# A strided load of 127 rows becomes one of 128 rows, and one row is replaced behind the flip

## The chip, the cores and the metric

The kernel runs on one core of a Trainium2 chip. The metric is the device time of one execution in microseconds (us), and lower is better. The program has five engines that run their own instruction streams: TensorE (PE in the profile, with PEld for its weight loads), VectorE (DVE), ScalarE (ACT), GpSimd (POOL) and SyncE (SP), which here only issues transfers.

## The reference

The reference takes `x` of shape (8, 3008, 256) and two weight matrices. It computes the real part of a two-dimensional discrete Fourier transform over the sequence (3008) and the channels (256) of each of the 8 batches, and puts the 24064 resulting rows through a two-layer network with an ELU between:

```python
X = np.fft.fft(np.fft.fft(x, axis=1), axis=2).real
h = X.reshape(24064, 256) @ w_in            # 256 x 2048
g = np.where(h > 0, h, np.exp(np.minimum(h, 0)) - 1)
out = g @ w_out                             # 2048 x 256
```

`x` is float32. The weights come as float64, and the kernel converts them itself, chunk by chunk, with integer and float operations on VectorE, ScalarE and GpSimd.

## The kernel before

The transform over the sequence is done as matrix products with cosine and sine tables (tiles `MC`). Since cosine is even and sine is odd, rows s and 3008 - s, and rows counted from the middle, 1504, are first added or subtracted ("folded"), so that about a quarter of the rows is left to multiply. The results go to the rings `Rr`, `Ir` and `Rb`, and the network reads its columns from there: matrix products into the PSUM tiles `H`, an ELU on DVE, ACT and POOL into `G`, and the second product into the four accumulators `pA` to `pD`. After the first batch this is one long stream of matrix products. The next batch's rows are loaded and folded underneath it.

The change lies in the load of batch 0, before that stream can begin. Four tiles `xl0` to `xl3` of 128 partitions hold six rows of 256 channels in each partition:

- `xl0` and `xl3` are read ascending from row 0 and from row 1504. Their first four rows per partition are called `x0a` and `x3a`, their last two `x0b` and `x3b`.
- `xl1` and `xl2` are read from the second half and from the first half of the sequence, and are to be used in descending order. Two of their six rows per partition, `x1b` and `x2b`, are gathered in descending order by GpSimd. Their four-row parts `x1a` and `x2a` are read in ascending order, and TensorE then turns the partitions round by a product with a flipped identity matrix (`flip`), function `turn`: the result is a PSUM tile `H`.

`first_folds` names the steps. `t3a`, `t3b`, `t0a` and `t0b` are the four turns: `t3*` turns parts of `xl2`, which belong to `xl3`, and `t0*` turns parts of `xl1`, which belong to `xl0`. `a` stands for rows 1 and 3 of a partition, `b` for rows 0 and 2. The mirrors `y3a`, `y3b`, `y0a`, `y0b` on DVE add the turned rows to `xl3` and `xl0` (channels reversed), and `y3c` and `y0c` do the same with the gathered rows. `Za`, `Zb` and `Zc` add `xl0` and `xl3`, `Zd` and `Ze` (GpSimd) subtract them, `ea` to `ec` fold the channels, and `x-odd1`, `R-odd1` and so on are the first products with the tables. `w0a` to `w0M` convert the first chunk of weights.

Why `x1a` has 127 rows: partition 127 of `xl1` would begin at row 3005 of batch 0 and hold rows 3005, 3006, 3007 and 3008. Row 3008 is row 0 of the next batch, where the fold wants row 0 of this batch. So `load_first` (line 696) loads 127 partitions on SP, and ScalarE's queue issues two small transfers for partition 127: three rows (3 KB) and row 0 (1 KB).

The order is written out by hand: the string `FRONT` lists the steps, and the events are sorted and emitted in that order. Each engine executes its own part of it in order. For SP the list gives

`x2a x3a fl x1a x0a x3b x0b m0c m0a m0b m0d w0g cc m1 pk w1g m2 w2g w5g u0g ...`

where `fl` is the flip matrix, `m*` are tables, `w*g` and `u*g` chunks of weights and `cc` and `pk` small tables. TensorE begins with 13 keep-warm products on zeros, then `t3b t3a t0a t0b`, then 11 more keep-warm products (`d3 d8`), then `x-odd1`. DVE's order is `y3b y3a y0a y3c y0c Za y0b ea`. The PSUM tag `H` has three buffers.

The framework gives the transfers of SP and ScalarE eight semaphores in turn. An issue therefore waits for the landing of the eighth such transfer before it. In the kernel before, `w0g` uses the semaphore of `x1a` and `cc` that of `x0a`.

Of the kernel before, what the change touches and what calls it, by code (L numbers as in the profile page):

```python
# [17 lines left out]
SEQ = 3008  # L18
ND = 256
# [162 lines left out]
def kernel(  # L182
# [7 lines left out]
    nc = tc.nc  # L190
# [26 lines left out]
    def xrows(b, row, step, n, rows=6):  # L217

        return bass.AP(
            tensor=xt,  # L220
            offset=x.offset + (b * SEQ + row) * ND,
            ap=[[step * ND, n], [1, rows * ND]],
        )
# [373 lines left out]
    def bank(tag):  # L597
        bufs = 3 if tag == "H" else 1
        return ppool.tile([128, 512], FP, tag=tag, bufs=bufs, name=tag)

    def mm(out_, lhsT, rhs, start, stop=True):
        pin(
            nc.tensor.matmul(  # L603
                out_, lhsT=lhsT, rhs=rhs, start=start, stop=stop, skip_group_check=True
            )
        )

    def vtt(o, a, b, op):
        pin(nc.vector.tensor_tensor(out=o, in0=a, in1=b, op=op))  # L609

    def gtt(o, a, b, op):
        pin(nc.gpsimd.tensor_tensor(out=o, in0=a, in1=b, op=op))  # L612

    def act(o, i, func=AF.Copy, **kw):
        pin(nc.scalar.activation(out=o, in_=i, func=func, **kw))  # L615
# [78 lines left out]
    def load_first(L, j, few):  # L694

        if few or j in (0, 3):
            L_loads[j, few]()
            return
        n = 128 if j == 2 else 127
        row = (HALF if j == 2 else SEQ) - 511  # L700
        nc.sync.dma_start(out=L[j][0:n, 2 * ND :], in_=xrows(0, row, 4, n, 4))
        if j == 1:
            for c, r, m in ((2, SEQ - 3, 3), (5, 0, 1)):
                nc.scalar.dma_start(
                    out=L[j][127:128, c * ND : (c + m) * ND],
                    in_=xrows(0, r, 4, 1, m),
                )

    def first_folds(L):

        flip = spool.tile([128, 384], FP, tag="side", bufs=2, name="flip")[:, 0:128]
        rows = [t.rearrange("p (m d) -> p m d", d=ND) for t in L]
        plus, minus = rows[1][:, ::-1], rows[2]
        eo = [
            [
                spool.tile(
                    [128, 768], FP, tag=f"{k}{1 + 2 * kodd}", bufs=1, name=k
                )
                for k in "eo"
            ]  # L720
            for kodd in range(2)
        ]
        ops = {}

        turned = {}

        def turn(j, m):
            ps = turned[j, m.start] = bank("H").rearrange("p (m d) -> p m d", d=ND)
            mm(ps, flip, rows[(1, 2)[j == 3]][:, ::-1][:, m], True)

        def mirror(j, m):
            own = rows[j]
            if m is rest:
                other = rows[(1, 2)[j == 3]][:, ::-1][:, m]
            else:
                other = turned[j, m.start]
            vtt(own[:, m, 1:], own[:, m, 1:], other[:, :, :0:-1], ALU.add)
            vtt(own[:, m, 0:1], own[:, m, 0:1], other[:, :, 0:1], ALU.add)

        def fold(kodd, ri, m, tt):  # L740
            src = minus if kodd else plus
            lo, hi = (
                t.rearrange("p m (d o) -> p m o d", o=2)
                for t in (src[:, m, 1:129], src[:, m, 255:127:-1])
            )
            o = eo[kodd][ri].rearrange("p (m o d) -> p m o d", o=2, d=64)[:, m]
            if ri:
                tt(o, lo, hi, ALU.subtract)
            else:
                tt(o, lo[:, :, ::-1], hi[:, :, ::-1], ALU.add)  # L750

        def edge(kodd, m, copy):
            src = minus if kodd else plus
            o = eo[kodd][0].rearrange("p (m o d) -> p m o d", o=2, d=64)[:, m]
            copy(o[:, :, 0, 63:64], src[:, m, 0:1])

        def vcopy(o, i):
            pin(nc.vector.tensor_copy(out=o, in_=i))

        def add(m):  # L760
            vtt(plus[:, m], rows[0][:, m], rows[3][:, m], ALU.add)

        def even(m):
            fold(0, 0, m, vtt)
            edge(0, m, vcopy)

        near, odd, even_, rest = slice(0, 4), slice(1, 4, 2), slice(0, 3, 2), slice(4, 6)
        every = slice(0, 6)
        for key, m in (("a", odd), ("b", even_), ("c", rest)):
            for j in (0, 3):  # L770
                if m is not rest:
                    ops[f"t{j}{key}"] = lambda j=j, m=m: turn(j, m)
                ops[f"y{j}{key}"] = lambda j=j, m=m: mirror(j, m)
            ops["Z" + key] = lambda m=m: add(m)
            ops["e" + key] = lambda m=m: even(m)
        ops["oab"] = lambda: fold(0, 1, near, vtt)
        ops["oc"] = lambda: fold(0, 1, rest, vtt)
        for key, c in (("Zd", slice(0, 3 * ND)), ("Ze", slice(3 * ND, 6 * ND))):
            ops[key] = lambda c=c: gtt(L[2][:, c], L[0][:, c], L[3][:, c], ALU.subtract)
        ops["em"] = lambda: fold(1, 0, every, vtt)  # L780
        ops["cm"] = lambda: edge(1, every, act)
        ops["om"] = lambda: fold(1, 1, every, gtt)
        ops["fl"] = lambda: nc.sync.dma_start(out=flip, in_=FL_dr.ap())

        def keep():
            d = state["x_odd"] = spool.tile([128, 6], FP, tag="xd", bufs=1, name="xd")
            act(d.unsqueeze(2), minus[:, :, 128:129])

        ops["xd"] = keep
        return eo, plus[:, :, 128], ops  # L790
# [209 lines left out]
    class Dft:  # L1000
# [16 lines left out]
        def copy(self):  # L1017

            M, h = self.M, (self.n + 1) // 2
            self.anti = spool.tile([128, NH], FP, tag="anti", bufs=2, name="anti")  # L1020
            act(self.anti[0:M, 0:h], self.even[0:M, h : 2 * h])
# [674 lines left out]
    exp_neg(warm)  # L1696
    L_first, L_loads = load_x(0)
    EO, x_first, ops = first_folds(L_first)

    R_even, I_even = (Dft(ri, 0, 0, EO[0][ri]) for ri in range(2))  # L1700
# [42 lines left out]
    for j in range(4):  # L1743
        for few in range(2):
            names[f"x{j}{'ab'[few]}"] = lambda j=j, few=few: load_first(L_first, j, few)
# [209 lines left out]
    for n in range(16):  # L1955
        j, k = divmod(n, 4)
# [65 lines left out]
    for b in range(2, NB):  # L2022
# [35 lines left out]
        for n in range(4):  # L2058
            ri, m = divmod(n, 2)
            rel(46 + n, 1.3, quarter_pairs, b, ri, 0, 1 + m)  # L2060
        for n, step in enumerate((43, 44, 45, 46, 51, 53)):
            ri, m = divmod(n, 3)
# [65 lines left out]
```

## Time and profile before

| what | value |
|---|---|
| median of 3 runs | 1931.41 us (1931.06 to 1931.83) |
| the profiled execution, its own time | 1932.27 us |
| span of its profile | 1930.5 us |
| TensorE, busy | 1902.0 us, 99% |
| VectorE, busy | 1465.3 us, 76% |
| GpSimd, busy | 1352.9 us, 70% |
| ScalarE, busy | 878.0 us, 45% |
| mean TensorE clock granted | 0.995 |

The profile is of one execution. Its times are counted from the start of the span; the execution's own time is 1.8 us longer than the span. "L603" is line 603 of the kernel, which for a product is the line of the helper `mm`; likewise all DVE additions carry L609 and all ACT operations L615, so steps are told apart by their tiles and shapes. "Idle before" is what the engine waited before an instruction, and the name behind the arrow is what ended the wait. "SPq" is SyncE's instruction stream, in which issues of transfers stand.

### The profile page before, as it was taken

Reading aid. Unit: us, or ns where it says so; the run is one execution under the profiler, and the core shown is the slowest. Engines: PE = TensorE matmul, PEld = TensorE weight load, DVE = VectorE, ACT = ScalarE, POOL = GpSimd, SP = SyncE. Lnnn points to the kernel's source line nnn. Section 1 sums busy time; section 2 is a strip of 40 time slices with the busy share of each in tenths; the row PEclk is TensorE's granted clock in tenths of the full one; section 3 lists DMA queues with packets and bytes.
Section 4 is the critical chain, followed back from the end, with each engine's and each line's share of the span. In section 5 each row is a group of like instructions: output and inputs, shape, how many; then the busy total and the mean of one; then the engine's idle time right before and its main releaser. Section 6 shows DMA issues by size and latency. Waiting matters only on the chain.

```text
span 1930.5 us, 27900 instructions
## 1 busy us (share of the span) xinstructions
PE 1902.0 (99%) x8966; PEld 1650.3 (85%) x8966; DVE 1465.3 (76%) x2789; ACT 878.0 (45%) x1710; POOL 1352.9 (70%) x1835
## 2 busy tenths in 40 slices
PE   5999999999999999999999999999999999999999
PEld 2788888888888888888888888888888888888887
DVE  3876667778787887878877887877877778767666
ACT  1774444444444444444444444444444444444443
POOL 1798767777677776877668786677766777556554
PEclk7999999999999999999999999999999999999999
DMA  5534421211011111110201111012110210100101
GB/s 193 188 20 29 43 47 36 57 36 32 16 33 43 32 40 20 35 44 20 44 15 46 38 25 39 12 42 49 30 27 12 56 20 17 17 12 12 22 10 25
DMA packets 278806, 73.87 MB, mean 38 GB/s; under 512 B 253891, under 2 KB 268998, under 8 KB 278660
## 3 DMA queue, kind: packets, MB, share of 16 engines
q1 hardware_dynamic: 270304, 62.69, 16.4%
q0 software_dynamic: 6176, 9.13, 1.5%
q8 instruction: 71, 1.16, 0.3%
q14 instruction: 75, 0.61, 0.1%
q10 hardware_dynamic: 2180, 0.27, 0.1%
HBM read 47.17 MB, written 24.80 MB: 37 GB/s over the span
## 4 chain that ended last, share of the span: by engine, by line
PE 96%; DVE 1%; DMA 1%; ACT 1%; SPq 1%; issue 0%; POOL 0%; ACTq 0%; DVEq 0%; POOLq 0%
PE H L603 37%; PE pB L603 17%; PE pC L603 17%; PE pD L603 17%; PE pA L603 9%; DMA xl<-in_x_dram 1%; SPq L276 1%; ACT G L615 0%; ACT Wsc L615 0%; DVE xl L609 0%; ACT pow L615 0%; POOL w L612 0%; DVE v L609 0%; PE M L603 0%; DVE pow L475 0%
## 5 line engine op out<-in xcount | busy, mean ns | idle before, releaser
L612 POOL TENSOR_TENSOR G<-G 128x256 f32<-128x256 f32 x1437 | 1046.0, 737 | 501.4 <-DVE G L1419 342.4
L615 ACT ACTIVATE G<-H 128x512 f32<-128x512 f32 x376 | 224.6, 597 | 917.8 <-DVE G L1403 917.8
L1389 DVE SCALAR_TENSOR_TENSOR E<-Rb,wex,H 128x256 f32<-128x256 f32 x752 | 327.9, 477 | 334.7 <-PE H L603 329.6
L603 PE MATMUL H<-Rr,Wsc 128*128 128x256 f32 x1504 | 387.3, 380 | 0.0
L603 PE MATMUL H<-Ir,Wsc 128*128 128x256 f32 x1504 | 386.6, 379 | 0.3 <-DVE E L1389 0.3
L603 PE MATMUL pC<-G,WT 128*128 128x256 f32 x1440 | 369.5, 379 | 0.0
L603 PEld LDWEIGHTS H<-Ir,Wsc 128*128 128x128 f32 x1504 | 278.4, 189 | 47.9 <-DVE E L1389 2.4
L603 PEld LDWEIGHTS H<-Rr,Wsc 128*128 128x128 f32 x1504 | 282.1, 190 | 40.7 <-issue 2.1
L603 PEld LDWEIGHTS pC<-G,WT 128*128 128x128 f32 x1440 | 273.6, 190 | 37.2
L1403 DVE SCALAR_TENSOR_TENSOR G<-E,H 128x512 f32<-128x512 f32 x376 | 257.2, 684 | 41.7 <-POOL G L612 11.5
L1419 DVE SCALAR_TENSOR_TENSOR G<-G,H 128x512 f32<-128x512 f32 x376 | 256.1, 681 | 39.5 <-ACT G L615 39.5
L1419 DVE SCALAR_TENSOR_TENSOR G<-M,G 128x512 f32<-128x512 f32 x376 | 257.2, 684 | 1.2 <-ACT M L615 1.2
L615 ACT ACTIVATE G<-G 128x512 f32<-128x512 f32 x376 | 233.5, 621 | 0.1
L603 PE MATMUL pD<-G,w 128*128 128x256 f32 x784 | 229.4, 379 | 0.0
L603 PE MATMUL pA<-G,w 128*128 128x256 f32 x784 | 229.4, 379 | 0.0
L603 PE MATMUL pB<-G,w 128*128 128x256 f32 x784 | 229.3, 379 | 0.0
L615 ACT ACTIVATE M<-G 128x512 f32<-128x512 f32 x376 | 223.9, 596 | 0.9 <-DVE G L1403 0.9
L615 ACT ACTIVATE M<-M 128x512 f32<-128x512 f32 x376 | 221.2, 588 | 0.1
L603 PE MATMUL pB<-G,WT 128*128 128x256 f32 x720 | 214.3, 379 | 0.0
L603 PE MATMUL pD<-G,WT 128*128 128x256 f32 x720 | 214.1, 379 | 0.0
L603 PEld LDWEIGHTS pA<-G,w 128*128 128x128 f32 x784 | 148.9, 190 | 20.6 <-DVE G L1419 0.3
L603 PEld LDWEIGHTS pB<-G,w 128*128 128x128 f32 x784 | 148.9, 190 | 20.4 <-PE H L603 0.2
(169 smaller groups left out, 1561.7 us busy)
## 6 DMA issues: line engine op xcount, KB each, us to landing
out_dram<-ot SPq DMA_DIRECT2D x496, 32.0 KB
xq<-in_x_dram SPq DMA_DIRECT2D x48, 94.0 KB
out_dram<-ot SPq DMA_DIRECT2D x256, 2.0 KB
Rb<-r SPq DMA_DIRECT2D x10, 376.0 KB
raw<-in_moe_w_in_dram SPq DMA_DIRECT2D x7, 512.0 KB
MC<-dft_mats SPq DMA_DIRECT2D x3, 943.5 KB
xl<-in_x_dram SPq DMA_DIRECT2D x5, 512.0 KB
xq<-in_x_dram SPq DMA_DIRECT2D x12, 192.0 KB
```

What stands on the lines that cost most here:

```text
L276: nc.sync.dma_start(out=L[j][:, 0 : 4 * ND], in_=xrows(b, row, 4, 128, 4))
L603: nc.tensor.matmul(out_, lhsT=lhsT, rhs=rhs, start=start, stop=stop, skip_group_check=True)
L612: pin(nc.gpsimd.tensor_tensor(out=o, in0=a, in1=b, op=op))
L615: pin(nc.scalar.activation(out=o, in_=i, func=func, **kw))
L1389: nc.vector.scalar_tensor_tensor(out=S.E[:, c], in0=Rb[:, cols(i)], scalar=wex[:, f : f + 1], in1=S.H[:, c], op0=ALU.mult, op1=ALU.add,)
L1403: nc.vector.scalar_tensor_tensor(out=two(S.G[:, 0:512])[:, :, ::-1], in0=two(S.E), scalar=2.0, in1=two(S.H), op0=ALU.mult, op1=ALU.subtract,)
L1419: nc.vector.scalar_tensor_tensor(out=o, in0=e, scalar=-1.0, in1=h, op0=ALU.add, op1=ALU.max)
```

## The change

`x1a` is loaded like `x2a`, with all 128 partitions by one transfer on SP. Partition 127's fourth row is then row 3008 of the batch sequence, which is row 0 of batch 1. The two small transfers on ScalarE's queue go away. After the flip that row lies in partition 0, first row group, of the PSUM tile that `t0b` writes. There ScalarE overwrites it with row 0 of batch 0 from `xl0`, before the mirror `y0b` reads the tile.

```diff
@@ load_first
-        n = 128 if j == 2 else 127
         row = (HALF if j == 2 else SEQ) - 511
-        nc.sync.dma_start(out=L[j][0:n, 2 * ND :], in_=xrows(0, row, 4, n, 4))
-        if j == 1:
-            for c, r, m in ((2, SEQ - 3, 3), (5, 0, 1)):
-                nc.scalar.dma_start(
-                    out=L[j][127:128, c * ND : (c + m) * ND],
-                    in_=xrows(0, r, 4, 1, m),
-                )
+        nc.sync.dma_start(out=L[j][:, 2 * ND :], in_=xrows(0, row, 4, 128, 4))
@@ first_folds, turn
             ps = turned[j, m.start] = bank("H").rearrange("p (m d) -> p m d", d=ND)
             mm(ps, flip, rows[(1, 2)[j == 3]][:, ::-1][:, m], True)
+            if j == 0 and m.start == 0:
+                act(ps[0:1, 0], rows[0][0:1, 0])
```

The rest of the program is the same, instruction by instruction on each engine. Since two transfers fewer take a semaphore, the turn of the eight moves by two: `m0a` now waits for `x2a`, `m0b` for `x3a`, `m0d` for `fl`, `w0g` for `x1a`, `cc` for `x0a`, `m1` for `x3b`, `w1g` for `m0c`, `m2` for `m0a` and `w2g` for `m0b`.

## The prediction

> **What bounds the kernel now.** I read the page first: the busy shares, the slices and the chain that ended last.
>
> ```profile
> PE 1902.0 (99%) x8966; PEld 1650.3 (85%) x8966; DVE 1465.3 (76%) x2789; ACT 878.0 (45%) x1710; POOL 1352.9 (70%) x1835
> PE   5999999999999999999999999999999999999999
> PEclk7999999999999999999999999999999999999999
> PE 96%; DVE 1%; DMA 1%; ACT 1%; SPq 1%; issue 0%; POOL 0%; ACTq 0%; DVEq 0%; POOLq 0%
> ```
>
> The whole is bound by TensorE, except in the first slice (48 us), which is half empty and where the granted clock is low. A microsecond saved before the stream of products starts shifts all of it, since the 96% of the chain behind it is products one after another. So I next asked for busy time in stretches of the beginning. The columns are stretch, length, busy time of PE, PEld, DVE, ACT and POOL, granted clock, DMA share and GB/s.
>
> ```profile
> 3.00:6.00 3.00, 3.00 (x9) 1.06 (x7) 0.00 (x0) 0.00 (x0) 0.96 (x1) 1.00 1.02 391
> 7.00:14.00 7.00, 1.45 (x4) 0.38 (x2) 1.42 (x4) 0.00 (x0) 0.00 (x0) 0.95 0.06 26
> 14.00:23.00 9.00, 0.00 (x0) 0.00 (x0) 0.00 (x0) 0.00 (x0) 0.00 (x0) 0.50 0.69 211
> 26.00:29.00 3.00, 0.00 (x0) 0.00 (x0) 0.00 (x0) 0.00 (x0) 0.00 (x0) 0.50 0.07 27
> 30.00:34.00 4.00, 4.00 (x7) 1.23 (x6) 2.43 (x7) 0.00 (x0) 0.19 (x1) 0.53 0.80 256
> 34.00:42.00 8.00, 7.27 (x31) 4.45 (x29) 7.86 (x15) 0.72 (x1) 3.88 (x2) 1.00 0.93 332
> 80.00:1930.00 1850.00, 1846.65 (x8758) 1613.25 (x8756) 1418.72 (x2690) 846.54 (x1651) 1322.88 (x1803) 1.00 0.17 31
> ```
>
> From 7 to 14 us and again from 26 to 29 us the transfers move 26 or 27 GB/s at a share of 0.06 or 0.07, which is one of 16 engines. All five compute engines stand still. The timelines of TensorE, SP and VectorE (start, length, instruction, idle before and what ended it) say who waits:
>
> ```profile
> 6.57 1.88 PE L603 MATMUL H<-xl,flip 128*128 128x512 f32 x4
> 29.49 3.75 PE L603 MATMUL H<-xl,flip 128*128 128x512 f32 x4 [21.04 <-DMA xl<-in_x_dram]
> 33.03 2.93 PE L603 MATMUL M<-zero 128*128 128x512 bf16 x11
> ...
> 2.22 0.33 SPq L701 DMA_DIRECT2D xl<-in_x_dram  x1
> 2.60 11.38 SPq L276 DMA_DIRECT2D xl<-in_x_dram  x1
> 29.37 0.39 SPq L403 DMA_DIRECT2D raw<-in_moe_w_in_dram  x1
> ...
> 8.49 1.42 DVE L609 TENSOR_TENSOR xl<-xl,H 128x510 f32<-128x510 f32 x4 [7.41 <-PE H L603]
> 31.57 0.76 DVE L609 TENSOR_TENSOR xl<-xl,H 128x510 f32<-128x510 f32 x2 [21.66 <-PE H L603]
> 32.24 2.02 DVE L609 TENSOR_TENSOR xl<-xl,xl 128x510 f32<-128x510 f32 x5
> 34.19 0.74 DVE L609 TENSOR_TENSOR xl<-xl,H 128x510 f32<-128x510 f32 x2
> ```
>
> t3b and t3a run at 6.57 us; t0a waits 21.04 us for a transfer of xl and starts at 29.49. That transfer is x1a, issued at 2.22: 508 KB, or 520 KB of a thousand bytes, at 27 GB/s are 19.3 us, which is the time from about 6.5 us, when the rest of what was issued has landed, to the DMA packets' last semaphore of this load at 28.95. The next issue on SP, x0a, takes 11.38 us, because part of it goes to the engine that is full. Even what lands elsewhere stays incomplete: of the later loads' packets the trace has 120 of 128 early and the last 8 only after 30 us. w0g is issued at 29.37, right after x1a landed, whose semaphore it uses. x2a, from the same line but with 128 rows, is in the tile before 6.57. The 22 us are thus x1a on one engine, and not a lack of bandwidth.
>
> **What the skill says.** "DMA: Bandwidth & Descriptors", section "Why a DMA increments its semaphore by 16 and not by 1", says that a transfer from SP is split over the largest k up to 16 that divides the slowest dimension of both sides, with 127 partitions giving 1 and 128 giving 16. The trace agrees: x1a moves at 27 GB/s, and 391 GB/s is moved with x2a and x3a in flight. The same page, "Queues, rings and completion order", says that on each DMA engine descriptors are consumed in ring order; the last 8 packets of each later load, after 30 us, agree. "TensorE: Matmul & The Clock Gate", part 1, says that the clock halves after about 3.4 us without work and needs as long of work to return; here it is 0.50 from 14 us on and 1.00 from 34. No price is taken from the skill.
>
> **The change part by part.**
>
> Removed: two issues on ScalarE's queue, 0.53 and 0.24 us at 0.75 and 1.38 us. ScalarE's next real work is at 40.13 us, so this is worth nothing; they land long before x1a.
>
> x1a on 16 engines: I add up what must move, at the 391 GB/s of 3 to 6 us. 1.41 MB had moved by 6.0 us (3 us at 80 GB/s, 3 at 391), so the line begins at 6.0 - 1.41/0.391 = 2.4 us. In MB of a thousand KB, with the gathers x1b and x2b beside the queue: x1a is complete at 2.16 MB, x0a at 2.69, x3b 2.95, x0b 3.21, m0a 3.79, m0d 4.18, w0g 4.70, m1 5.86, w1g 6.41, m2 7.37, w2g 7.90. (The trace of before moved 7.9 MB up to 44 us, where SP's next batch starts.) That gives landings at 7.9, 9.3, 9.9, 10.6, 12.1, 13.1, 14.4, 17.4, 18.8, 21.3 and 22.6 us. From landing to the product it took 0.54 us before (28.95 to 29.49). The turn of eight semaphores holds nothing up: each issue needs a landing several microseconds before the queue runs dry (m0a needs x2a, w0g needs x1a at 7.9, w2g needs m0b at about 12.6).
>
> TensorE: t0a can start at the end of t3a, 8.45 us, or at 7.9 + 0.5; it ends at 9.4, since at full clock four passes took 1.88 (before: 3.75 at half clock). t0b ends at 10.3. DVE's y0a needs x0a, 9.3 + 0.5 = 9.8 us, and starts there instead of at 31.57. y3c needs x3b at 10.4, y0c x0b at 11.1; with 0.7 us for each mirror they start at 10.5 and 11.2, so they wait for nothing. Za ends at 12.5 instead of 34.26. The shift is 21.8 us.
>
> Does what follows keep it? All of it between 32 and 78 us stands in the chain as DVE, PE, ACT and POOL, without a transfer. Each need, moved by 21.8, against its landing plus 0.5: m0a 35.80 to 14.0 against 12.6; w0g 39.68 to 17.9 against 14.9; m1 42.52 to 20.7 against 17.9; w1g 43.62 to 21.8 against 19.3; w2g 46.66 to 24.9 against 23.1. The slack is 1.4 to 3 us. Behind that, SP was held before by the conversion of the first chunk, to 43.2 us, so its later issues move with the compute; the queue drains at 22.6 where the moved schedule begins to fill it at 44.2 - 21.8 = 22.4: 0.2 us late.
>
> The added copy on ScalarE: the nearest row is the same operation between SBUF tiles,
>
> ```profile
> L615 ACT ACTIVATE xl<-xl 1x256 f32<-1x256 f32 x1 | 0.4, 399 | 0.0
> ```
>
> so 0.4 us, from 10.3 (t0b) to 10.8. Its reader y0b comes after Za at 12.5 in DVE's order, so y3c, y0c and Za hide it. Without that cover it would cost 0.4 plus a hand-over, 0.5 us. The copy adds a wait at the head of ScalarE's stream; queued behind it is the first conversion step, at 40.13 before and 18.3 moved. Writing to PSUM isn't shown here for this shape; I bound it by 0.2 and 0.6 us (a 128x6 copy took 0.215, a 128x512 one out of PSUM 0.597), both hidden. x0's reload for batch 1 now also waits for this copy, at about 51 us before, 30 moved: nothing.
>
> Sum: -21.8 + 0.2 = -21.6, at most -22.2 (y0a at 9.4, with x0a in time), on 1932.27, the profiled execution: 1910.7. That execution is 0.86 above the median, so the median becomes 1909.8; I say 1910.0.
>
> **The rivals.**
>
> Transfers become the bound. If the packets flow at 256 GB/s, as in the stretch 30 to 34, and not at 391, x0b is in at 2.4 + 3.21/0.256 + 0.5 = 15.4 (4.2 late) and w2g at 33.7 instead of 24.9, 8.8 late: the gain shrinks to 13 us, 1918.4. At 332 (34 to 42) it is 1.8 less: 1911.8. For it: the stretch 14 to 23 shows 211. Against: there one engine of 16 was out and SP itself stalled, and 44 to 62 us holds 383 with the same kinds of loads.
>
> The load doesn't spread, because something other than the count keeps it on one engine: 1931.4, no change. Against: x2a, same line, same strides.
>
> Slower: the dense stretch starts with a clock below 1.00, for instance because the long rest at half clock was what allowed it. 1% of clock on 1846.65 us of products is 18.5 us, so the gain is gone when the mean falls under 0.988; at 0.98 the time is 1931.4 - 21.4 + 37 = 1947. Against: 1.00 is granted over all of 80 to 1930 us.
>
> The copy is late after all (y0b waits): gain less 0.5 to 1, 1910.8.
>
> **How the numbers follow.** Full shift 0.75 (its own range 1908.5 to 1912.5), late copy 0.06, transfers as bound 0.14 (1912 to 1925, most of it below 1918), doesn't spread 0.03, slower 0.02. The forecast is 1910.0. The range 1908.0 to 1917.0 holds the first two and over half of the third; below lies the bound -22.2 with the runs' spread of 0.4. About 0.2% (3.9 us) is what a measurement of this kernel can tell from no change: faster 0.95, same 0.03, slower 0.02.
>
> **What would show it.** Right: SP's issues 2 to 8 within a few us without the 11 us one; DMA near 390 GB/s from 3 to 22 us with no stretch of 26; t0a directly behind t3a near 8.5 us at clock 1.00; y0a near 9.8; ScalarE's copy of 1x256 near 10.5 with y0b behind Za; x-odd1 near 14; the dense stretch 21 to 22 us earlier and the same length. Wrong: t0a again after 20 us (it doesn't spread); DVE or PE waiting on transfers of MC or raw between 10 and 25 us (bandwidth); a clock below 1.00 after 34 us.

## The result, and the profile after

The changed kernel takes 1913.61 us (median of 6 runs, 1911.99 to 1916.05), against 1931.39 us (1931.06 to 1931.83) for the kernel before. The ratio is 0.9908 with a 95% interval of 0.9896 to 0.9921: 0.9% faster. The profiled execution took 1911.99 us, its span is 1910.2 us; against the profiled execution before that is 20.3 us less.

The page of the changed kernel: the slices of TensorE and its clock, and the chain by engine.

```profile
PE   8999999999999999999999999999999999999999
PEclk9999999999999999999999999999999999999999
PE 97%; DVE 1%; ACT 1%; DMA 0%; issue 0%; POOL 0%; SPq 0%; ACTq 0%; DVEq 0%; POOLq 0%
```

The first slice went from 5 to 8 tenths, and the low clock in it is gone. The shares of DMA and of SP's queue in the chain have fallen from 1% each to below half a percent. One piece of DMA is left in the chain's first 110 us, the wait up to the landing of x0a (start, length):

```profile
2.62 8.42 DMA xl<-in_x_dram
```

Busy time by stretch (length, then PE, PEld, DVE, ACT and POOL, granted clock, DMA share, GB/s):

```profile
3.00:6.00 3.00, 3.00 (x9) 1.05 (x7) 0.00 (x0) 0.00 (x0) 0.96 (x1) 1.00 0.94 339
6.00:10.00 4.00, 3.23 (x9) 1.16 (x7) 1.30 (x4) 0.00 (x0) 0.00 (x0) 1.00 0.98 359
10.00:14.00 4.00, 3.66 (x15) 1.35 (x13) 2.99 (x10) 0.38 (x1) 0.64 (x1) 1.00 1.04 398
18.00:22.00 4.00, 4.00 (x18) 2.92 (x17) 3.90 (x11) 1.08 (x3) 0.00 (x0) 1.00 1.02 415
60.00:1910.00 1850.00, 1846.25 (x8756) 1613.06 (x8754) 1417.66 (x2689) 845.86 (x1650) 1322.35 (x1803) 1.00 0.16 31
```

No stretch of 26 GB/s is left. From 3 to 22 us the transfers run without a hole, and the dense stretch is as long as it was: 1846.25 us of products in 1850, against 1846.65. The timelines of TensorE, SP, ScalarE and VectorE:

```profile
6.71 1.95 PE L603 MATMUL H<-xl,flip 128*128 128x512 f32 x4 [0.21 <-DMA flip<-flip_mats]
9.22 1.98 PE L603 MATMUL H<-xl,flip 128*128 128x512 f32 x4 [0.56 <-DMA xl<-in_x_dram]
13.94 1.51 PE L603 MATMUL pD<-MC,xl 128*128 128x377 f32 x4 [0.34 <-DVE xl L609]
17.51 1.54 PE L603 MATMUL pB<-MC,e 128*128 128x377 f32 x4 [2.06 <-DVE e L753]
...
2.62 0.43 SPq L276 DMA_DIRECT2D xl<-in_x_dram  x1
9.20 0.39 SPq L403 DMA_DIRECT2D raw<-in_moe_w_in_dram  x1
...
11.24 0.38 ACT L615 ACTIVATE H<-xl 1x256 f32<-1x256 f32 x1 [9.01 <-PE H L603]
...
11.13 0.75 DVE L609 TENSOR_TENSOR xl<-xl,H 128x510 f32<-128x510 f32 x2 [1.01 <-DMA xl<-in_x_dram]
11.80 2.02 DVE L609 TENSOR_TENSOR xl<-xl,xl 128x510 f32<-128x510 f32 x5
13.74 0.74 DVE L609 TENSOR_TENSOR xl<-xl,H 128x510 f32<-128x510 f32 x2
```

t0a starts at 9.22 us instead of 29.49, the issue of x0a takes 0.43 us instead of 11.38, w0g is issued at 9.20 instead of 29.37, and y0a starts at 11.13 instead of 31.57. y0b (13.74) follows y3c, y0c and Za without a gap, and ScalarE's copy (0.38 us) had ended 2 us before. From y0a on the chain of waits is the old one, moved. Its first long run of products without a break, in the kernel before and in the changed one:

```profile
78.38 1.97 PE H L603 x8
```

```profile
57.95 1.97 PE H L603 x8
```

The shift is 20.44 us at y0a and still 20.43 us here. Nothing was lost on the way.

### The profile page after: what moved, and what is told of

It reads as the page before. It is cut to its first block, busy times and chain, and to the rows that moved or that the text cites. A ratio compares the mean times of both kernels' runs of the same rounds, so it can differ in the third digit from the quotient of the medians.

```text
span 1910.2 us, 27901 instructions
## 1 busy us (share of the span) xinstructions
PE 1900.1 (99%) x8966; PEld 1649.5 (86%) x8966; DVE 1464.5 (77%) x2789; ACT 878.1 (46%) x1711; POOL 1352.8 (71%) x1835
## 4 chain that ended last, share of the span: by engine, by line
PE 97%; DVE 1%; ACT 1%; DMA 0%; issue 0%; POOL 0%; SPq 0%; ACTq 0%; DVEq 0%; POOLq 0%
PE H L603 38%; PE pB L603 17%; PE pC L603 17%; PE pD L603 17%; PE pA L603 9%; DMA xl<-in_x_dram 0%; ACT G L615 0%; ACT Wsc L615 0%; DVE xl L609 0%; ACT pow L615 0%; POOL w L612 0%; DVE v L609 0%; PE M L603 0%; DVE pow L475 0%; DVE u L609 0%
```

## The experiments

My theory: the whole gain is the spread of x1a over 16 engines in place of one, and the copy behind the flip costs nothing. Rivals: the copy stands on the path; something other than the count of rows held the load up; only one engine is bad and any other count is as good. What I had not foreseen was a spread of the runs of 4 us, where the kernel before has 0.8; the second half of the experiments is about that.

**The copy alone.** The kernel before with the two lines of the copy added:

```diff
             mm(ps, flip, rows[(1, 2)[j == 3]][:, ::-1][:, m], True)
+            if j == 0 and m.start == 0:
+                act(ps[0:1, 0], rows[0][0:1, 0])
```

> The kernel before with ScalarE's copy behind the flip added, everything else kept (127 rows on one engine, the two small loads on ScalarE's queue). Theory (the gain is all in the load, the copy is hidden): 1931.4 us, within 0.5, t0a still at about 29.5 us. Rival (the copy's wait on x0a and t0b stands on the path): 0.4 to 1 us slower, y0b of VectorE with a wait for ScalarE in front of it.

Measured: 1931.70 us (12 runs), ratio 1.0, interval 0.9991 to 1.0008; t0a at 28.85 us, nearly as late as before (29.49). The copy by itself does nothing.

**The load alone.** The changed kernel without those two lines.

> The changed kernel without ScalarE's copy: the row that belongs to the next batch stays in, so one row of the fold is another one. Theory (copy hidden behind y3c, y0c and Za): the time of the changed kernel, 1912 to 1916 us, y0b at 13.7 us as there. Rival (the copy costs): 0.4 to 1 us less than the changed kernel.

Measured: 1912.77 us (1911.58 to 1913.55, 4 runs), inside the spread of the changed kernel. The median is 0.8 us below that of the changed kernel's first six runs, as the rival would have it, but 0.1 above that of the four further runs told of below (1912.69), so the trace has to decide. From the first of VectorE's five additions (y3c, y0c, Za) to y0b it is 1.95 us here (11.34 to 13.29) and 1.94 us with the copy (11.80 to 13.74), so the copy isn't in front of y0b. It costs nothing that these runs can tell.

**127 rows on 15 engines.** No row of the next batch and no copy; the small loads on ScalarE's queue stay:

```diff
-        nc.sync.dma_start(out=L[j][0:n, 2 * ND :], in_=xrows(0, row, 4, n, 4))
+        cuts = (0, n) if j == 2 else (0, 120, n)
+        for p, q in zip(cuts, cuts[1:]):
+            nc.sync.dma_start(
+                out=L[j][p:q, 2 * ND :], in_=xrows(0, row + 4 * p, 4, q - p, 4)
+            )
```

> The kernel before with the 127 rows in two transfers of 120 and 7 rows on SP, the small loads of ScalarE's queue kept, no copy behind the flip. Theory (one engine for 127 rows is the whole cause; 120 rows take 15 engines and 7 rows take 7): nearly the changed kernel, 1912 to 1916 us, t0a at 9 to 10 us. Rival (the cause is the partial tile or the small loads on ScalarE's queue, and not the count of engines): 1931 us, t0a near 29 us.

Measured: 1913.59 us (1912.49 to 1915.08), ratio 0.9907 (0.9890 to 0.9923). The same 127 rows, cut at 120, give the gain of the change. The partial tile and ScalarE's small loads are thereby ruled out; whether any cut would do is asked next. t0a starts at 10.45 us, a little later than expected:

```profile
10.45 1.96 PE L603 MATMUL H<-xl,flip 128*128 128x512 f32 x4 [1.32 <-DMA xl<-in_x_dram]
```

**118 and 9 rows, 124 and 3 rows.** The same edit with 118 or 124 in place of 120, for two and for four engines. The transfers are the same in number and order as with 120, so only the place of the cut differs.

> As the split before, but 118 and 9 rows: 118 is twice 59, so the large part should go to two engines. Theory: 59 packets of 4 KB per engine at 0.15 us are 8.9 us behind about 5.5 us, plus 1.2 us for the gathers' share, so t0a at about 16 us, y0a at 17 to 17.5 us, 6 us behind the changed kernel: 1918 to 1921 us. Rival (only whether the count is 127 or not matters): as 120 and 7, 1912 to 1916 us.

> The kernel before with the 127 rows in two transfers of 124 (four times 31) and 3 rows, the small loads kept. Theory (the largest divisor up to 16 sets the engines): from 59 packets on an engine landing at about 18.1 us and 127 at 28.95, a packet costs 0.16 us, so 31 land at 13.6 us, t0a at about 14.1 us, at half clock since TensorE has been idle for 6 us; y0a at 16 us, 5 us behind the changed kernel: 1916 to 1918.5 us. Rival (anything but one or two engines is as good as sixteen): 1912 to 1914 us.

Measured: 1921.58 us (1921.30 to 1921.70) and 1919.19 us (1918.82 to 1919.78). TensorE's turns t0a and t0b with 118, then with 124 rows:

```profile
18.61 3.66 PE L603 MATMUL H<-xl,flip 128*128 128x512 f32 x4 [10.59 <-DMA xl<-in_x_dram]
```

```profile
16.32 3.75 PE L603 MATMUL H<-xl,flip 128*128 128x512 f32 x4 [7.74 <-DMA xl<-in_x_dram]
```

| rows in the large part | its landings in the trace | t0a starts, us | y0a starts, us | median, us |
|---|---|---|---|---|
| 127 (the copy alone) | 1 | 28.85 | 30.93 | 1931.70 |
| 118 | 2 | 18.61 | 20.70 | 1921.58 |
| 124 | 4 | 16.32 | 18.41 | 1919.19 |
| 120 | 15 | 10.45 | 11.90 | 1913.59 |
| 128 (changed kernel, once more) | 16 | 8.86 | 10.62 | 1912.69 |

The trace records the landings of a transfer one by one, and their number tells how many engines carried it: it is 1, 2, 4, 15 and 16, each time the largest divisor of the row count up to 16 (the small parts of 9, 3 and 7 rows have 9, 3 and 7). With 118 rows there is also a stretch in which little but this load moves, at a share of two engines of 16 and at about twice the 26 GB/s of the kernel before:

```profile
14.00:18.00 4.00, 0.00 (x0) 0.00 (x0) 0.00 (x0) 0.00 (x0) 0.00 (x0) 0.50 0.14 56
```

Both rivals fall: 118, 124 and 120 rows lie between 127 and 128, in the order of their divisors and not in that of their size. And a microsecond by which y0a is late is nearly a microsecond of the total: from 127 to 118 rows y0a comes 10.2 us earlier and the total falls by 10.1; from there to 124 it is 2.3 and 2.4; from there to 128 it is 7.8 and 6.5 (7.1 from profiled run to profiled run). My size for two and four engines was wrong: t0a came 2.6 and 2.2 us after the times I had expected, and both totals lie 0.6 to 0.7 us above my ranges. With 124 rows the stretches of busy time show why:

```profile
6.00:10.00 4.00, 1.96 (x4) 0.68 (x4) 1.38 (x4) 0.00 (x0) 0.00 (x0) 1.00 1.01 283
10.00:14.00 4.00, 0.00 (x0) 0.00 (x0) 0.04 (x1) 0.00 (x0) 0.00 (x0) 0.63 1.02 220
```

All 16 engines count as busy (share 1.02), but they move 220 GB/s together, where the changed kernel moves 398 in the same stretch with loads of the same kinds. A packet takes longer: those of 3 KB took 0.24 us at the median in this stretch, and 0.12 in the changed kernel. So the 0.16 us per packet of 4 KB that I had used was too little.

**The spread of the runs.** The changed kernel ran at a mean granted clock of 1.000 in the run of 1911.99 us and of 0.999 in the five others. I supposed that the idle 2.06 us of TensorE in front of R-odd1 (17.51 us above) sometimes takes the clock down. In the kernel before this gap is 0.73 us:

```profile
35.80 1.43 PE L603 MATMUL pD<-MC,xl 128*128 128x377 f32 x4
37.96 1.53 PE L603 MATMUL pB<-MC,e 128*128 128x377 f32 x4 [0.73 <-DVE e L758]
```

R-odd1 starts 6.39 us behind y0a there and 6.38 in the changed kernel, so VectorE sets it in both. But x-odd1 starts 4.23 us behind y0a there and 2.81 in the changed kernel, because the turns and the keep-warm products before it no longer run wholly or in part at half clock (3.75 and 2.93 us then, 1.98 and 2.56 now). That opens the gap.

The changed kernel was run again beside one with that gap filled:

```diff
-        ... Za d3 d8 x-odd1 y0b ea R-odd1 ...
+        ... Za d3 d8 x-odd1 d9 y0b ea R-odd1 ...
```

> The changed kernel once more, beside the next three. Its runs so far spread over 4 us (1912.0 to 1916.0) where the kernel before spreads over 1. Theory: TensorE stands still for 2.06 us in front of R-odd1, and [...] this takes the clock to one half for one window or two,[...] which costs 1.7 or 3.4 us; so the runs fall into groups at about 1911.9, 1913.6 and 1915.3, and a granted clock of 1.000 goes with the lowest. Rival: the spread is in the landing of the first loads, then it goes with no difference in the clock.

> The changed kernel with 9 more keep-warm products ([...]1.9 us) between x-odd1 and R-odd1, into the idle 2.06 us. Theory (the clock falls in that gap): all runs near 1911.9, spread under 1 us, granted clock 1.000. Rival (the spread comes from the landing of the loads): median 1913.6 and spread of 3 to 4 us as without them.

Measured: again without the fill 1911.98, 1911.58, 1913.40 and 1913.67 us, the first two with a clock of 1.000 and the others with 0.999: the two lower groups that were expected. With the fill 1911.36, 1911.57, 1912.04 and 1911.87 us, all at 1.000. TensorE with the fill:

```profile
13.34 1.50 PE L603 MATMUL pD<-MC,xl 128*128 128x377 f32 x4 [0.40 <-DMA MC<-dft_mats]
14.68 2.12 PE L603 MATMUL M<-zero 128*128 128x512 bf16 x9
16.87 1.54 PE L603 MATMUL pB<-MC,e 128*128 128x377 f32 x4
```

R-odd1 now follows the fill directly, and no run is at 0.999 any more. Of the changed kernel, with and without the copy, 9 of 14 runs were at 0.999; of the fill and of the two versions below, in which the gap is shorter or filled, none of 12. Then the opposite, the 11 keep-warm products in front of x-odd1 taken away:

```diff
-        ... Za d3 d8 x-odd1 y0b ...
+        ... Za x-odd1 y0b ...
```

> The changed kernel without the 11 keep-warm products between t0b and x-odd1, so that TensorE is idle from about 10.9 to 13.7 us and again from 15.2 to 17.2 us. Theory (gaps of TensorE in the front take the clock down[...]): the clock is at 0.50 for a stretch in every run or nearly every run, the profile shows that stretch, and the time is 1913.5 to 1917 us. Rival (the 0.999 of some runs has nothing to do with gaps): 1911.6 to 1913.7 us as the changed kernel, some runs at 1.000.

Measured: 1913.93 us (1913.16 to 1915.24), the clock between 0.997 and 0.998 in all four runs. Two of the four times lie in the rival's range as well; it is the clock that decides. The profile shows the fall. Busy time by stretch, and TensorE's first products after the gap:

```profile
10.00:14.00 4.00, 1.23 (x3) 0.50 (x2) 3.57 (x10) 0.38 (x1) 1.24 (x1) 0.86 1.05 401
14.00:16.00 2.00, 2.00 (x4) 0.67 (x2) 1.97 (x2) 0.00 (x0) 2.00 (x2) 0.50 1.09 439
20.00:22.00 2.00, 2.00 (x8) 2.00 (x7) 2.00 (x5) 0.00 (x0) 0.00 (x0) 0.50 0.96 382
...
13.36 2.85 PE L603 MATMUL pD<-MC,xl 128*128 128x377 f32 x4 [2.77 <-DVE xl L609]
16.91 2.88 PE L603 MATMUL pB<-MC,e 128*128 128x377 f32 x4 [0.70 <-DVE e L753]
```

The four products of R-odd1 take 2.88 us instead of 1.54. So a gap in the front can take the clock down, and with the gap filled the spread was gone. What isn't seen directly is a fall in the changed kernel itself: its profiles are of runs at 1.000, so that its 2.06 us take the clock down is inferred. The spread in the landing of the loads, the rival, is there too but smaller: in the changed kernel's two profiles y0a starts at 11.13 and 10.62 us, and a run of the 120-row split took 1913.56 us at a clock of 1.000. One run stays unexplained: 1916.05 us at 0.999. By my estimate 0.001 of the clock over 1912 us is 1.9 us, and this run is 4.1 us above the lowest.

**A faster version.** Why does TensorE have that gap? R-odd1 waits for a copy of two columns on VectorE, at 15.81 us in the changed kernel, that takes 1.65 us beside GpSimd's subtractions Zd and Ze; its two sisters later take 0.17. VectorE and GpSimd in the changed kernel:

```profile
15.81 1.65 DVE L753 COPY e<-xl 128x2 f32<-128x2 f32 x1
17.37 0.68 DVE L609 TENSOR_TENSOR xl<-xl,xl 128x512 f32<-128x512 f32 x1
18.54 0.17 DVE L753 COPY e<-xl 128x2 f32<-128x2 f32 x1
...
13.36 4.07 POOL L612 TENSOR_TENSOR xl<-xl,xl 128x768 f32<-128x768 f32 x2 [9.23 <-DMA MC<-dft_mats]
```

I put these three copies on ScalarE, once alone and once with three keep-warm products:

```diff
-            edge(0, m, vcopy)
+            edge(0, m, act)
```

> The changed kernel with the three small edge copies behind the channel folds ea, eb and ec on ScalarE instead of VectorE. In the changed kernel the first one takes 1.65 us on VectorE beside GpSimd's Zd and Ze, where the second and third take 0.17. Theory: R-odd1 starts at about 16.2 instead of 17.5 us and the median falls by 0.5 to 1.5 us, partly by the shorter gap of TensorE. Rival: the next VectorE step, Zb, is held by GpSimd in its place, and nothing is gained beyond 0.3 us.

> The edge copies on ScalarE as in the run before, and 3 keep-warm products (0.65 us) between x-odd1 and R-odd1. Theory: 1910.5 to 1911.5 us with a spread under 1 us, the fastest of all. Rival: as the changed kernel, 1913.6.

Measured: 1911.47 us (1911.31 to 1911.82) and 1911.25 us (1911.07 to 1912.06), ratio to the kernel before 0.9896 for both (0.9879 to 0.9912), the clock at 1.000 in all eight runs. VectorE and ScalarE around the first copy, with the copies on ScalarE alone:

```profile
14.05 1.37 DVE L609 TENSOR_TENSOR e<-xl 128x256 f32<-128x256 f32 x1
15.45 2.18 DVE L609 TENSOR_TENSOR xl<-xl,xl 128x512 f32<-128x512 f32 x1
17.67 0.43 DVE L609 TENSOR_TENSOR e<-xl 128x256 f32<-128x256 f32 x1
...
15.45 0.21 ACT L615 ACTIVATE e<-xl 128x2 f32<-128x2 f32 x1 [4.20 <-DVE e L609]
```

R-odd1 starts at 15.71 us, but Zb now takes 2.18 us in place of 0.68 and ends at 17.63, where the changed kernel's second profile has 17.71. The rival was right on that: VectorE's hold-up only changes its victim. It was wrong on the gain, which is 1.2 us by the medians. I put this down mainly to the clock, as with the fill, and to about half a microsecond from the shorter list of VectorE; the medians of the fill (1911.72) and of this version lie too close together to show the latter. By their medians the filled gap, the moved copies and both together lie 1.0 to 1.4 us below the changed kernel beside them (1912.69), and all twelve of their runs lie within 1 us, at 1911.1 to 1912.1. Which of the three is the fastest these runs don't tell.

## Why the prediction was right or wrong

It forecast 1910.0 us in a range of 1908.0 to 1917.0; 1913.61 is inside, and outside the likeliest case's own range (1908.5 to 1912.5). That the median is inside is in part luck: the range was that wide for a late copy and for transfers as the bound, and what filled it was the clock. The difference of 3.6 us is accounted for below.

- *x1a sits on one engine, and on 16 it is done at once*: right. x1a left the place of the bound; the row with 120 shows that it is the divisor, and the dose of 1, 2, 4, 15 and 16 engines orders the starts of t0a. One reading beside it was wrong: the 19.3 us of x1a at 27 GB/s are not the time from 6.5 to 28.95 us, which is 22.4 us. x1a was not yet alone then; the gathers' last landings are recorded at 9.18 and 10.60 us. No term of the gain used it.
- *The sum of bytes at 391 GB/s*: right in kind, too optimistic in size. y0a was to start at 9.8 us and started at 11.13 in the profiled run (10.3 to 10.7 in the profiles of the six other runs with the 128-row load). In the sum this is 1.3 of the 3.6 us: the profiled execution came to 1911.99 where the sum had 1910.7. Two terms failed. One is the rate: 339 and 359 GB/s in 3 to 6 and 6 to 10 us, not 391; at these, and 81 GB/s before 3 us, the 2.69 MB that the sum has up to the end of x0a have moved at 10.0 us instead of 9.3. But the run without the keep-warm products in front of x-odd1 moved 395 and 392 GB/s, and its y0a still started at 10.37. The other is the end of a load: the trace records the 16 landings of x0a in the profiled run between 9.75 and 11.04 us, and y0a follows the last of them, while the sum lets all 16 engines finish together. What spreads them is open.
- *The later deadlines keep their slack*: right for the chain, wrong for m0a. The chain's shift at 57.95 us is the shift at y0a to 0.01 us, and no wait on a transfer stands in the chain after y0a. But x-odd1 at 13.94 (I had 14.0) is a hit by luck: y0a came 1.3 us late, and x-odd1 came 1.4 us closer behind it than before. m0a, which was to have 1.4 us to spare, had none: its last landing is recorded at 13.81 us, and in the trace with the fill x-odd1's last wait is for `MC`, as it is in the changed kernel's second profile. This cost nothing, since R-odd1 waits for VectorE.
- *ScalarE's copy, 0.4 us, hidden behind y3c, y0c and Za*: right. It took 0.38 us and had 2.1 us to spare; taken away or added, it moves nothing.
- *The clock at 1.00 from t0a on*: wrong for most runs, and the step the prediction did not take. I checked that t0a would find a warm TensorE and that d3 and d8 fill the time before x-odd1, but not that the gap in front of R-odd1, 0.73 us in the kernel before, would grow to 2.06 us. Five runs of six are at 0.999. The Trainium skill, "TensorE: Matmul & The Clock Gate", part 1, has the clock fall after about 3.4 us without work; here filling 2.06 us was enough to end the 0.999. Without the keep-warm products the clock fell after about 2.3 us without work (an estimate from the mean of 0.86 over 10 to 14 us, with TensorE idle from 10.6), so the measurement decides.
- *The profiled execution stands 0.86 us above the median*: I carried that over from the kernel before. Here the profiled execution is the fastest of six, 1.6 us under the median; it alone of the six is at 1.000. Together with the forecast's rounding that is the other 2.3 us of the 3.6.
- *The rivals*: transfers as the bound did not come true: the rate falls behind the forecast only until about 10 us, and then it is above (398, 415). Nor did "doesn't spread" or "slower". The clock rival had the right place in mind, TensorE's clock, but the wrong stretch: 1.00 is granted over all the dense stretch, and the one fall that was seen, without the keep-warm products, is in the front.

## What to carry to other kernels

A DMA share that stays near 1/16 while every compute engine waits was one transfer on one engine here: look for a load whose row count has no good divisor up to 16, and cut or pad it. A cut (120 and 7) was as good as a padded load with a repair within the spread of the runs, and needs no repair behind the flip, though it keeps the two small loads of the last partition. When such a stall is gone, look at the small gaps of TensorE that are left: with one of 2 us most runs read a lower clock, and a few products on zeros cost nothing and made the runs agree.

## What the runs showed of the hardware that I had not expected

With 4 engines carrying the large load, all 16 engines counted as busy and moved 220 GB/s in 10 to 14 us (226 GB/s at a share of 0.84 with 2 engines); with 128 rows they moved 398. So beside a load on few engines the others were slower too, and not only those behind it on the same engine. With 120 and 7 rows, on 15 and 7 engines, the rate was 255 in 6 to 10 us at a share of 1.01, so it need not be the fewness. Why, no run here tells.

The stretches in which the traces have the clock at one half before the end are 20.48 us long (the kernel before, and with the copy alone) or 10.24 us (118 rows, 124 rows, and without the keep-warm products), and a stretch of 6.83 us at full clock stands in front of each: all are multiples of 3.41 us. One such piece at half clock would bring the mean over 1912 us to 0.999 and cost 1.7 us, about what lies between the runs at 1.000 and most of those at 0.999. This is an estimate; no such piece was seen in a trace of the changed kernel. The record of the clock begins only at about 6 us, and what the views give as 1.00 before that isn't full speed: the first products on zeros start 0.43 us apart in the changed kernel, the 11 at 11.04 us 0.22 apart.

The same two-column copy on VectorE took 1.65 us beside GpSimd's two 128x768 subtractions and 0.17 without, and the addition put in its place took 2.18 instead of 0.68. That GpSimd is the cause is argued from the times alone (the hold-up ends when GpSimd's work ends, at 17.4 us in the changed kernel); it was not tried with GpSimd's work moved. And not every VectorE addition was held: y0b, which reads one operand from the PSUM tile `H`, ran beside the first of the two subtractions in 0.74 us, like y0a before them (0.75).
